# Halo matmuls in 32-row quarters, the first channel piece decoded between the first sums, and the token weights stored by SP behind the later loads

## The chip, the cores and the metric

The kernel runs on one core of a Trainium2 chip. The metric is device time in microseconds; before the change the median of three runs is 2021.88 us (2021.09 to 2022.40). Lines such as L522 are lines of the kernel before; the change moves later lines down, so the same statement can have another number in the changed kernel.

## What is computed

Eight sequences of 4096 tokens with 192 channels go through a causal convolution with seven taps (one softmax-normalized filter for each of eight heads of 24 channels), then through two residual products: over the tokens (4096 to 256 to 4096) and over the channels (192 to 1536 to 192). The weights arrive as 64-bit floats.

```python
w = softmax(weight)                                  # 8 heads x 7 taps
out = einsum('hk,bskhg->bshg', w, windows_of(x))     # causal: six zero rows ahead
xt = out.transpose(0, 2, 1)
h = np.maximum(xt @ w_tok1, 0.0) @ w_tok2
u = out + h.transpose(0, 2, 1)
h2 = np.maximum(u @ w_ch1, 0.0) @ w_ch2
return u + h2
```

## The kernel before

The eight sequences are worked in five groups (1, 1, 2, 2, 2). Only the first sequence and its function `stage1_first` are touched. A row block is 128 tokens; a sequence has 32 of them, in four chunks of eight (`x0`, `xc`).

**Convolution of the first sequence.** For every head a 128 x 128 matrix `band` multiplies a row block (L522), and a second matrix `corner` multiplies the row block ahead of it (L523): only the last six rows of that block, the halo, meet weights other than zero. Both products go over all 128 rows. A chunk therefore takes 16 matmuls in plain float32 (a float32 matmul is two records in the trace). Chunks 1 to 3 load nine row blocks for eight, the first being the halo's. `conv_out` (L525) copies the sums from PSUM to `xc` on ScalarE.

**Decoding.** A 64-bit weight is turned into float32 by an Abs on ScalarE (L196) and four operations on VectorE (L198, L199, L202, L205); pieces that are used in two parts (high and low) get a cast on ScalarE (L211) and a subtraction on VectorE (L212). Sixteen pieces are loaded by SP in a fixed order: eight of the first token weights (t1, kept in `tops`), the first piece of the second token weights (t2 piece 0), three thirds of the first channel weights (w1), three of the second (w2, kept as `w2f`), and t2 piece 1. The raw pieces live in six buffers, so a load waits until the last VectorE operation (L205) on the piece that held its buffer.

**Products of the first sequence.** `mix` (L453) sums `xc` times t1 into two PSUM accumulators; `mix1_done` (L382, L383) makes their parts `h1`; `first_mix` is the call of `mix2` (L920 to L922, sums on VectorE at L935) on the first four row blocks, which needs t2 piece 0; `first_transposed` makes the operand `own` (L984 to L990); `first_channel1` (L1080, Relu L1092) needs w1, `first_channel2` (L1098) w2. The next `mix2` (L924, L925) needs t2 piece 1. The order of all this is written out by hand at the end of `stage1_first` (L572 to L622).

**Stores of that stage.** `xc` goes to DRAM by SP (L538); the decoded t1 goes to DRAM as `t1d` by GpSimd's queue (L445), ahead of `first_channel1`; the next sequences read it from there (L712). SP's queue works in program order: a transfer that waits holds all behind it. The first load of the next sequence (`raw`, L648) takes memory that `tops` held, so it waits for those stores.

Of the kernel before, what the change touches and what calls it, by code (L numbers as in the profile page):

```python
# [139 lines left out]
def conv_mixer_kernel(ctx: ExitStack, tc: tile.TileContext, x, weight, w_tok1, w_tok2, w_ch1, w_ch2, out):  # L140
# [6 lines left out]
    P = 128  # L147
# [241 lines left out]

    def stage1_first(pe, p0, pd, late, load_u, load_next, after, thirds, hooks):
        b = GROUPS[0][0]
        NC = 8
        chunks = [range(s0, s0 + NC) for s0 in range(0, NJ, NC)]
# [24 lines left out]
        t1s = t1d.rearrange("(j p) m -> p j m", p=P)  # L420

        band = p0.tile([P, H, P], F32, name="band")
        corner = p0.tile([P, H, P], F32, name="corner")
        nc.gpsimd.memset(corner, 0.0)

        homes = [(pe if c else p0).tile([P, NC + 1, D], F32, name=f"x0_{c}") for c in range(len(chunks))]
        xcs += [p0.tile([P, NC, D], F32, name=f"xc0_{c}") for c in range(len(chunks) - 1)]
        tops = [p0.tile([P, TJ * JT], F32, name=f"t1_{i}") for i in range(NJ // TJ)]

        def x0_load(c):  # L430
            x0 = homes[c]
            x0s.append(x0)
            j0 = chunks[c].start
            if c == 0:
                nc.gpsimd.memset(x0[:, 0, :], 0.0)
                nc.sync.dma_start(out=x0[:, 1:], in_=xt[:, 0:NC])
            else:
                nc.sync.dma_start(out=x0, in_=xt[:, j0 - 1:j0 + NC])

        def t1_job(i):  # L440
            src = w_tok1.rearrange("(j p) m -> p j m", p=P)[:, quads[i].start:quads[i].stop]
            return dict(src=src, shape=[TJ, JT], top=lambda: tops[i])

        def t1_store(i):
            nc.gpsimd.dma_start(  # L445
                out=t1s[:, quads[i].start:quads[i].stop], in_=tops[i].rearrange("p (j m) -> p j m", m=JT)
            )

# [34 lines left out]
        def make_band():  # L483


            def moved(out, off, hs):
                at0 = P - off
                nc.tensor.matmul(out=out, lhsT=turn[:, at0:at0 + P], rhs=band_r[:, hs], start=True, stop=True)

            halves = [slice(h, h + H2) for h in (0, H2)]  # L490
            for hs in halves:
                v = products.rearrange("p (h c) k -> p h c k", c=BC)
                nc.vector.tensor_tensor(
                    out=v, in0=ones.unsqueeze(1).to_broadcast([BR, H2, BC, K]),
                    in1=cw[:BR, hs].unsqueeze(2).to_broadcast([BR, H2, BC, K]), op=ALU.mult,
                )
                nc.vector.tensor_reduce(
                    out=band_r[:, hs].rearrange("p h c -> p (h c)"), in_=products, axis=AX.X, op=ALU.add
                )
            for hs in halves:  # L500
                ps = ps_x.tile([P, P // BC, H2, BC], F32, name="ps_x")
                for b0 in range(P // BC):
                    moved(ps[:, b0], b0 * BC - HALO, hs)
                nc.scalar.copy(out=band[:, hs].rearrange("p h (b c) -> p b h c", c=BC), in_=ps)
                ps = ps_x.tile([P, H2, BC], F32, name="ps_x")
                moved(ps, P - HALO, hs)
                nc.scalar.copy(out=corner[:, hs, 0:BC], in_=ps)
                if hs.start == 0:
                    keep_busy(9)

        def conv_mm(m):
            c, part = m // 2, m % 2
            x0 = x0s[c]
            n = NC
            for h2 in range(part * H // 4, (part + 1) * H // 4):
                ps = ps_x.tile([P, TT], F32, name="ps_x")
                convs.setdefault(m, []).append((h2, ps))
                for i in range(2):
                    h = 2 * h2 + i
                    o = ps[:, i * n * G:(i + 1) * n * G].rearrange("p (j g) -> p j g", g=G)  # L520
                    hs = slice(h * G, (h + 1) * G)
                    nc.tensor.matmul(out=o, lhsT=band[:, h], rhs=x0[:, 1:, hs], start=True, stop=False)  # L522
                    nc.tensor.matmul(out=o, lhsT=corner[:, h], rhs=x0[:, :n, hs], start=False, stop=True)  # L523

        def conv_out(m):  # L525
            c, part = m // 2, m % 2
# [15 lines left out]
        def begin(n):  # L542
            chains_a.append(dec.a(sts[n], jobs[n]["top"]() if "top" in jobs[n] else None))
# [28 lines left out]
        for n in range(nj - 1):  # L572
            if n + 2 < nj:
                begin(n + 1)
# [6 lines left out]
            if n in (len(quads) - 1, len(quads)):  # L581
                woven(chains.pop(0))
            woven(*chains, split(n - 2) if n > 1 and "top" not in jobs[n - 2] else [])
            if n + 2 == nj:
                begin(n + 1)
            for fn in work.get(n, ()):
                fn()
            if n not in (0, 6, 9):
                next_load()
            if n == 1:  # L590
                x0_load(3)
            if n == 8:
                for c in (3, 0, 1, 2):
                    xc_store(c)
            if n == 7:
                load_u(xcs[0])
            if n == 9:
                late()
        n = nj - 1
        mix1_done(0, accs)  # L600
        woven(split(n - 2))
        hooks[0]()
        hooks[1]()
        woven(chains_a[n - 1][2:], chains_a[n][:2])
# [295 lines left out]
    QB = 32  # L900
    NQ = P // QB

    def mix2(gi, q, t2, u, at_once=False, turned=None):
        nb = len(GROUPS[gi])
        n = nb * D

# [6 lines left out]
        for j in range(TJ):  # L913
# [150 lines left out]
    def first_next(xc):  # L1064
        first["next"] = first_load(xc, TJ)

    def first_mix():
        mix2(0, 0, *first["u"], at_once=True)

    def first_transposed():  # L1070
        first["abc"] = transposed(first["u"][1])
# [98 lines left out]
        queue.dma_start(out=dst[:, js.start:js.stop], in_=osb[:, js.start:js.stop])  # L1170

    hp = None
    pe_ctx, p0_ctx, pd_ctx, ht_ctx = (ExitStack() for _ in range(4))
    pe = pe_ctx.enter_context(tc.tile_pool(name="pe", bufs=1))
    pd = pd_ctx.enter_context(tc.tile_pool(name="pd", bufs=1, side="right"))
    p0 = p0_ctx.enter_context(tc.tile_pool(name="p0", bufs=1, side="right"))

    def first_late():
# [6 lines left out]
    def first_done():  # L1185
# [6 lines left out]

    thirds = [range(p, p + NP // 3) for p in range(0, NP, NP // 3)]
    stage1_first(
        pe, p0, pd, first_late, first_u, first_next, first_done, thirds,
        [first_mix, first_transposed] + [lambda p=p: first_channel1([p]) for p in range(NP)],
    )
    pd_ctx.close()
    t2sp.append(t2s_ctx.enter_context(tc.tile_pool(name="t2s1", bufs=1, side="right", reuse_waits="tile")))

# [203 lines left out]
```

## Time and profile before

| | |
|---|---|
| median of 3 runs | 2021.88 us |
| the profiled execution: its own time, its span | 2020.89 us, 2019.1 us |
| TensorE busy | 2004.4 us, 99% of the span |
| TensorE busy in the first 140 us | 129.81 us |
| VectorE busy in the first 140 us | 114.71 us |
| granted TensorE clock | 1.00 throughout |
| all DMA engines, first 140 us | share 0.79, 257 GB/s |

How to read the lines in the prediction: a timeline row is start, duration, engine, line, operation, output<-inputs, shapes, number merged (x), and in brackets the idle time of the engine ahead of it and what ended it. A row of the chain of waits is start, duration and what the program's end waited on there. A row of the table by windows is the stretch, its length, busy time and number of instructions of PE, weight loads, DVE, ACT, POOL, then the clock, the DMA share (1.0 is all 16 engines; rounding takes it a little above) and GB/s. "SPq" is SP issuing a transfer.

### The profile page before, as it was taken

Reading aid. Unit: us, or ns where it says so; the run is one execution under the profiler, and the core shown is the slowest. Engines: PE = TensorE matmul, PEld = TensorE weight load, DVE = VectorE, ACT = ScalarE, POOL = GpSimd, SP = SyncE. Lnnn points to the kernel's source line nnn. Section 1 sums busy time; section 2 is a strip of 40 time slices with the busy share of each in tenths; the row PEclk is TensorE's granted clock in tenths of the full one; section 3 lists DMA queues with packets and bytes.
Section 4 is the critical chain, followed back from the end, with each engine's and each line's share of the span. In section 5 each row is a group of like instructions: output and inputs, shape, how many; then the busy total and the mean of one; then the engine's idle time right before and its main releaser. Section 6 shows DMA issues by size and latency. Waiting matters only on the chain.

```text
span 2019.1 us, 44729 instructions
## 1 busy us (share of the span) xinstructions
PE 2004.4 (99%) x18667; PEld 1859.3 (92%) x18667; DVE 1506.1 (75%) x3008; ACT 777.5 (39%) x1280; POOL 216.9 (11%) x380
## 2 busy tenths in 40 slices
PE   9899999999999999999999999999999999999999
PEld 9789999999999999998999999999999999999998
DVE  8799998998758998857985689556666666666664
ACT  4676554544333434324333334233233222333322
POOL 0100000001211011100111100111111010011110
PEclk9999999999999999999999999999999999999999
DMA  9855446455455567324654435433223232333310
GB/s 306 285 160 164 137 156 203 153 170 176 138 152 142 160 191 204 115 77 123 170 162 116 116 83 157 148 87 85 54 72 83 71 85 69 77 85 85 85 49 17
DMA packets 280089, 260.93 MB, mean 129 GB/s; under 512 B 188624, under 2 KB 227280, under 8 KB 279888
## 3 DMA queue, kind: packets, MB, share of 16 engines
q1 hardware_dynamic: 257360, 179.80, 31.6%
q0 software_dynamic: 22528, 78.27, 12.9%
q8 instruction: 148, 2.42, 0.5%
q14 instruction: 53, 0.43, 0.1%
HBM read 146.60 MB, written 71.30 MB: 108 GB/s over the span
## 4 chain that ended last, share of the span: by engine, by line
PE 89%; DVE 5%; DMA 3%; SPq 1%; ACT 1%; issue 1%; POOL 0%; ACTq 0%; DVEq 0%
PE ps_x L1080 36%; PE ps_x L1139 23%; PE ps_x L1156 12%; PE ps_x L1157 5%; PE ps_x L959 2%; DVE xc L660 2%; PE ps_a L767 2%; PE ps_a L768 2%; PE ps_a L769 2%; DMA dec_raw<-in_moe_w_tok_dram 1%; DVE hl L1122 1%; PE ps_x L927 1%; PE ps_x L924 1%; PE ps_x L929 1%; PE ps_x L928 1%; PE ps_a L763 1%
## 5 line engine op out<-in xcount | busy, mean ns | idle before, releaser
L1121 ACT ACTIVATE hh<-ps_x 128x512 fp32r<-128x512 f32 x756 | 411.1, 596 | 838.9 <-PE ps_x L1080 838.8
L1122 DVE SCALAR_TENSOR_TENSOR hl<-ps_x,hh 128x512 fp32r<-128x512 f32 x756 | 484.5, 684 | 190.5 <-ACT hh L1121 188.9
L1139 PE MATMUL ps_x<-w,hh 64*128 64x384 f32 x3360 | 481.3, 355 | 0.0
L1139 PE MATMUL ps_x<-w,hl 64*128 64x192 f32 x3360 | 421.2, 247 | 0.0
L660 DVE SCALAR_TENSOR_TENSOR xc<-raw,cw,xc 128x384 f32<-128x384 f32 (+1 forms) x768 | 388.0, 559 | 8.5 <-ACT xc L658 8.5
L1156 PE MATMUL ps_x<-w,hh 128*128 128x384 f32 x1344 | 387.6, 360 | 0.0
L1080 PE MATMUL ps_x<-other,w_hi 64*128 64x512 f32 x1296 | 337.2, 388 | 0.0
L1157 PE MATMUL ps_x<-w,hl 128*128 128x192 f32 x1344 | 336.5, 250 | 0.0
L1080 PE MATMUL ps_x<-own_hi,w_hi 64*128 64x512 f32 x1440 | 332.6, 392 | 1.6 <-ACT own_hi L989 0.6
L1080 PE MATMUL ps_x<-own_lo,w_hi 64*128 64x512 f32 x1440 | 326.1, 387 | 0.1
L1080 PE MATMUL ps_x<-own_hi,w_lo 64*128 64x512 f32 x1440 | 325.7, 387 | 0.0
L1139 PEld LDWEIGHTS ps_x<-w,hl 64*128 64x128 f32 x3360 | 321.3, 188 | 0.9
L1139 PEld LDWEIGHTS ps_x<-w,hh 64*128 64x128 f32 x3360 | 315.4, 184 | 0.9
L1157 PEld LDWEIGHTS ps_x<-w,hl 128*128 128x128 f32 x1344 | 256.6, 191 | 0.0
L1080 PEld LDWEIGHTS ps_x<-other,w_hi 64*128 64x128 f32 x1296 | 235.5, 184 | 22.3
L1156 PEld LDWEIGHTS ps_x<-w,hh 128*128 128x128 f32 x1344 | 252.3, 188 | 0.4 <-DVE hl L1122 0.4
L1080 PEld LDWEIGHTS ps_x<-own_hi,w_hi 64*128 64x128 f32 x1440 | 212.7, 184 | 32.5 <-issue 4.6
L1080 PEld LDWEIGHTS ps_x<-own_lo,w_hi 64*128 64x128 f32 x1440 | 218.4, 184 | 25.3 <-ACT own_lo L990 0.5
L1080 PEld LDWEIGHTS ps_x<-own_hi,w_lo 64*128 64x128 f32 x1440 | 218.2, 184 | 25.2
L1080 PE MATMUL ps_x<-other,w_lo 64*128 64x512 f32 x648 | 181.5, 386 | 0.0
L1147 DVE TENSOR_TENSOR osb<-ps_x,osb 128x192 f32<-128x192 f32 x420 | 150.1, 357 | 25.7 <-DVE osb L1147 0.9
L1145 DVE TENSOR_TENSOR osb<-ps_x,u 128x192 f32<-128x192 f32 x140 | 49.7, 355 | 135.0 <-PE ps_x L1139 135.0
(164 smaller groups left out, 2421.7 us busy)
## 6 DMA issues: line engine op xcount, KB each, us to landing
raw<-in_x_dram SPq DMA_DIRECT2D x56, 672.0 KB, 7.3
t<-t2d SPq DMA_DIRECT2D x64, 512.0 KB, 5.8
u<-xcd SPq DMA_DIRECT2D x62, 384.0 KB, 7.3
xcd<-xc POOLq DMA_DIRECT2D x28, 768.0 KB, 8.0
t<-t1p SPq DMA_DIRECT2D x32, 512.0 KB, 4.5
out_dram<-osb POOLq DMA_DIRECT2D x36, 384.0 KB, 3.4
out_dram<-osb SPq DMA_DIRECT2D x27, 384.0 KB, 3.3
t2d<-stage SPq DMA_DIRECT2D x16, 512.0 KB, 4.9
```

Of the source, the lines that this page charges most:

```text
L660: nc.vector.scalar_tensor_tensor(out=dst, in0=src, scalar=cw[:, h, k:k + 1], in1=dst, op0=ALU.mult, op1=ALU.add)
L767: nc.tensor.matmul(out=ps, lhsT=wh, rhs=xh, start=a, stop=False)
L768: nc.tensor.matmul(out=ps, lhsT=wh, rhs=xl, start=False, stop=False)
L769: nc.tensor.matmul(out=ps, lhsT=wl, rhs=xh, start=False, stop=z)
L1080: nc.tensor.matmul(out=ps, lhsT=w1[w][rows, t[h][2][c], p * P:(p + 1) * P], rhs=t[h][v][rows, c], start=n == 0, stop=n == len(prods) - 1,)
L1121: nc.scalar.activation(out=h["hh", f], in_=ps, func=AF.Relu)
L1122: nc.vector.scalar_tensor_tensor(out=h["hl", f], in0=ps, scalar=0.0, in1=f32(h["hh", f]), op0=ALU.max, op1=ALU.subtract)
L1139: nc.tensor.matmul(out=ps[:, :m], lhsT=h[part, f][ks, ts], rhs=w2[ks, f, :m], start=n == 0 and part == "hh", stop=z and part == "hl",)
L1145: nc.vector.tensor_tensor(out=rows(osb[:, j]), in0=rows(pss[0][:, :D]), in1=tokens(u, i)[:, j], op=ALU.add)
L1147: nc.vector.tensor_tensor(out=osb[:, j], in0=v, in1=osb[:, j], op=ALU.add)
L1156: nc.tensor.matmul(out=ps[:, :2 * D], lhsT=h["hh", f][:, ts], rhs=w2[:, f, :], start=n == 0, stop=False)
L1157: nc.tensor.matmul(out=ps[:, :D], lhsT=h["hl", f][:, ts], rhs=w2[:, f, :D], start=False, stop=z)
```

## The change

Four things are changed, all for the first sequence:

1. The halo has a tile of its own: `halo` holds at partitions 32g to 32g+5 the last six rows of every preceding row block, for head pair g. Four transfers on ScalarE's queue fill it from x (6 x 31 runs of 48 floats each). Chunks load eight row blocks. The `corner` matrices stand in the same quarters, and the eight halo matmuls of a chunk use six rows of one quarter each, four to a round, and follow the eight band matmuls of the chunk.
2. The decode of the first third of w1 no longer stands ahead of `mix1_done`: the loop ends one piece earlier, and the four VectorE operations on that third are put between the four sums of `first_mix` (`between`). The later thirds move back accordingly.
3. The stores of t1 to `t1d` are issued by SP, behind the load of t2 piece 1; they were on GpSimd's queue ahead of `first_channel1`.
4. `tops` and three of the `xc` tiles are in a pool of their own (`p1`), closed after the stage; the stores of `xc` go in the order 0, 3, 1, 2.

```diff
+        halo = p0.tile([P, NJ, 2 * G], F32, name="halo")
+        nc.gpsimd.memset(halo[:, 0], 0.0)
+        for g in range(NQ):
+            nc.scalar.dma_start(
+                out=halo[g * QB:g * QB + HALO, 1:], in_=xt[P - HALO:, :NJ - 1, 2 * g * G:2 * (g + 1) * G]
+            )
...
-                nc.sync.dma_start(out=x0, in_=xt[:, j0 - 1:j0 + NC])
+            nc.sync.dma_start(out=x0, in_=xt[:, chunks[c].start:chunks[c].stop])
...
         def t1_store(i):
-            nc.gpsimd.dma_start(
+            nc.sync.dma_start(
...
-                    nc.tensor.matmul(out=o, lhsT=band[:, h], rhs=x0[:, 1:, hs], start=True, stop=False)
-                    nc.tensor.matmul(out=o, lhsT=corner[:, h], rhs=x0[:, :n, hs], start=False, stop=True)
+                    nc.tensor.matmul(out=sums(ps, i), lhsT=band[:, h], rhs=x0[:, :, hs], start=i == 0, stop=False)
+            if part:
+                for i in range(2):
+                    for g, ps in convs[m - 1] + convs[m]:
+                        rs = slice(g * QB, g * QB + HALO)
+                        nc.tensor.matmul(
+                            out=sums(ps, i), lhsT=corner[rs, g, i],
+                            rhs=halo[rs, chunks[c].start:chunks[c].stop, i * G:(i + 1) * G], start=False, stop=i == 1,
+                        )
...
+        woven(chains_a[nt][2:])
+        late()
+        woven(split(nt))
         mix1_done(0, accs)
-        woven(split(n - 2))
-        hooks[0]()
+        hooks[0](list(chains_a[nt + 1]))
+        woven(split(nt + 1))
+        begin(nt + 2)
+        next_load()
+        woven(chains_a[nt + 2][:2])
         hooks[1]()
...
+        woven(chains_a[nt + 3][2:])
+        next_load()
+        woven(split(nt + 3))
         for i in range(len(quads)):
             t1_store(i)
...
+                if between:
+                    between.pop(0)()
```

The order on VectorE from the end of t2 piece 0 (`dec_top_432`, shape 128x1024) to the first operations on `own_lo`; `dec_top_448` and `dec_top_476` are the first two thirds of w1, L383 is `mix1_done`, L935 the sums of `first_mix`. Before:

```order
L198 TENSOR_SCALAR dec_top_448<-dec_top_448 128x768
L205 SCALAR_TENSOR_TENSOR dec_top_432<-early_raw_353,dec_top_432 128x1024
L199 TENSOR_SCALAR dec_top_448<-dec_top_448 128x768
L202 SCALAR_TENSOR_TENSOR dec_top_448<-dec_raw_376,dec_top_448 128x768
L198 TENSOR_SCALAR dec_top_476<-dec_top_476 128x768
L212 TENSOR_TENSOR t2s_91<-dec_top_432,t2s_91 128x2x512
L205 SCALAR_TENSOR_TENSOR dec_top_448<-dec_raw_376,dec_top_448 128x768
L199 TENSOR_SCALAR dec_top_476<-dec_top_476 128x768
L383 SCALAR_TENSOR_TENSOR h1_486<-ps_a0_133,h1_486 128x192
L383 SCALAR_TENSOR_TENSOR h1_486<-ps_a1_134,h1_486 128x192
L212 TENSOR_TENSOR w1_lo_69<-dec_top_448,w1_hi_68 128x3x256
L935 TENSOR_TENSOR u_446<-ps_x_504,u_446 128x192
```

The same place now (`dec_top_442` is t2 piece 0, `dec_top_458` the first third of w1, L950 the sums):

```order
L205 SCALAR_TENSOR_TENSOR dec_top_442<-early_raw_363,dec_top_442 128x1024
L212 TENSOR_TENSOR t2s_91<-dec_top_442,t2s_91 128x2x512
L383 SCALAR_TENSOR_TENSOR h1_492<-ps_a0_142,h1_492 128x192
L383 SCALAR_TENSOR_TENSOR h1_492<-ps_a1_143,h1_492 128x192
L198 TENSOR_SCALAR dec_top_458<-dec_top_458 128x768
L950 TENSOR_TENSOR u_456<-ps_x_500,u_456 128x192
L199 TENSOR_SCALAR dec_top_458<-dec_top_458 128x768
L950 TENSOR_TENSOR u_456<-ps_x_509,u_456 128x192
L202 SCALAR_TENSOR_TENSOR dec_top_458<-dec_raw_386,dec_top_458 128x768
L950 TENSOR_TENSOR u_456<-ps_x_518,u_456 128x192
L205 SCALAR_TENSOR_TENSOR dec_top_458<-dec_raw_386,dec_top_458 128x768
L950 TENSOR_TENSOR u_456<-ps_x_527,u_456 128x192
```

Six operations on w1 that stood ahead of L383 stand behind it now: four between the sums, two (L198 and L199 of the second third) behind them.

The order on SP from the load of t2 piece 1 (`dec_raw`, 128x2x1024) to the first loads for the next sequence (`raw`, then `t1` read back from `t1d`). Before:

```order
L232 DMA dec_raw_605<-in_moe_w_tok2_dram 128x2x1024
L648 DMA raw0_759<-in_x_dram 128x14x96
L648 DMA raw1_762<-in_x_dram 128x14x96
L712 DMA t1_765<-t1d_72 128x512
L712 DMA t1_767<-t1d_72 128x512
```

And now:

```order
L232 DMA dec_raw_607<-in_moe_w_tok2_dram 128x2x1024
L446 DMA t1d_72<-t1_0_134 128x4x256
L446 DMA t1d_72<-t1_1_135 128x4x256
L446 DMA t1d_72<-t1_2_136 128x4x256
L446 DMA t1d_72<-t1_3_137 128x4x256
L446 DMA t1d_72<-t1_4_138 128x4x256
L446 DMA t1d_72<-t1_5_139 128x4x256
L446 DMA t1d_72<-t1_6_140 128x4x256
L446 DMA t1d_72<-t1_7_141 128x4x256
L661 DMA raw0_770<-in_x_dram 128x14x96
```

The eight stores stand between the last load of the stage and `raw` on the same queue; from the loads of t1 from `t1d` on, the order on every engine is that of before.

More of the change, by code (lines that the diff above doesn't have):

```diff
@@ L388, in mix1_accs, with stage1_first @@
         return [ps_a.tile([P, TT], F32, name=f"ps_a{kc}") for kc in range(KC)]
-    def stage1_first(pe, p0, pd, late, load_u, load_next, after, thirds, hooks):
+    def stage1_first(pe, p0, p1, pd, late, load_u, load_next, after, thirds, hooks):
         b = GROUPS[0][0]
@@ L504, in make_band @@
                 nc.scalar.copy(out=band[:, hs].rearrange("p h (b c) -> p b h c", c=BC), in_=ps)
-                ps = ps_x.tile([P, H2, BC], F32, name="ps_x")
-                moved(ps, P - HALO, hs)
-                nc.scalar.copy(out=corner[:, hs, 0:BC], in_=ps)
+                ps = ps_x.tile([P, 2, 2, BC], F32, name="ps_x")
+                gs = range(hs.start // 2, hs.stop // 2)
+                for n, g in enumerate(gs):
+                    moved(ps[:, n], g * QB, slice(2 * g, 2 * (g + 1)))
+                nc.scalar.copy(out=corner[:, gs.start:gs.stop, :, 0:BC], in_=ps)
                 if hs.start == 0:
@@ L571, in stage1_first @@
         }
-        for n in range(nj - 1):
-            if n + 2 < nj:
-                begin(n + 1)
+        nt = len(quads)
+        for n in range(nt + 1):
+            begin(n + 1)
             if n == 1:
@@ L579, in stage1_first @@
             chains = [chains_a[n - 1][2:] if n else [], chains_a[n][:2]]
-            if n in (len(quads) - 1, len(quads)):
+            if n >= nt - 1:
                 woven(chains.pop(0))
-            woven(*chains, split(n - 2) if n > 1 and "top" not in jobs[n - 2] else [])
-            if n + 2 == nj:
-                begin(n + 1)
+            woven(*chains)
             for fn in work.get(n, ()):
                 fn()
-            if n not in (0, 6, 9):
+            if n not in (0, 6):
                 next_load()
@@ L901, in conv_mixer_kernel, with mix2 @@
     NQ = P // QB
-    def mix2(gi, q, t2, u, at_once=False, turned=None):
+    def mix2(gi, q, t2, u, at_once=False, turned=None, between=()):
         nb = len(GROUPS[gi])
@@ L1065, in first_next, with first_mix @@
         first["next"] = first_load(xc, TJ)
-    def first_mix():
-        mix2(0, 0, *first["u"], at_once=True)
+    def first_mix(between):
+        mix2(0, 0, *first["u"], at_once=True, between=between)
     def first_transposed():
@@ L1172, in conv_mixer_kernel @@
     hp = None
-    pe_ctx, p0_ctx, pd_ctx, ht_ctx = (ExitStack() for _ in range(4))
+    pe_ctx, p0_ctx, p1_ctx, pd_ctx, ht_ctx = (ExitStack() for _ in range(5))
     pe = pe_ctx.enter_context(tc.tile_pool(name="pe", bufs=1))
     pd = pd_ctx.enter_context(tc.tile_pool(name="pd", bufs=1, side="right"))
+    p1 = p1_ctx.enter_context(tc.tile_pool(name="p1", bufs=1, side="right"))
     p0 = p0_ctx.enter_context(tc.tile_pool(name="p0", bufs=1, side="right"))
@@ L1194, in conv_mixer_kernel @@
     stage1_first(
-        pe, p0, pd, first_late, first_u, first_next, first_done, thirds,
+        pe, p0, p1, pd, first_late, first_u, first_next, first_done, thirds,
         [first_mix, first_transposed] + [lambda p=p: first_channel1([p]) for p in range(NP)],
     )
+    p1_ctx.close()
     pd_ctx.close()
```

36 lines of the change are left out of this document (13 added, 23 removed).

## The prediction, made before the changed kernel was run

> **What bounds the kernel now.** The page comes first, then a table by windows to see where TensorE (PE) waits at all.
>
> ```profile
> PE 2004.4 (99%) x18667; PEld 1859.3 (92%) x18667; DVE 1506.1 (75%) x3008; ACT 777.5 (39%) x1280; POOL 216.9 (11%) x380
> ...
> core 0: us, PE busy (x) PEld busy (x) DVE busy (x) ACT busy (x) POOL busy (x), PEclk, DMA share, GB/s
> 3.20:43.10 39.90, 39.90 (x259) 39.11 (x258) 34.15 (x41) 15.38 (x25) 1.91 (x3) 1.00 1.05 346
> 13.20:55.50 42.30, 42.06 (x257) 41.54 (x256) 37.12 (x42) 19.84 (x32) 0.82 (x1) 1.00 1.06 321
> 55.48:88.09 32.61, 27.38 (x189) 21.92 (x189) 24.88 (x35) 18.86 (x29) 7.47 (x10) 1.00 0.84 303
> 110.50:116.20 5.70, 2.91 (x24) 2.30 (x20) 5.05 (x11) 3.74 (x7) 0.00 (x0) 1.00 0.32 92
> 116.20:140.00 23.80, 23.80 (x181) 22.38 (x183) 21.38 (x52) 17.42 (x24) 0.75 (x1) 1.00 0.50 158
> ```
>
> PE is busy for 99% of the span; what it lacks lies almost wholly ahead of 116 us. From there PE never stops, so a change in the first stage is worth what it moves the moment at which PE has the first sequence's operands. From 13 to 55 us PE is full, but so are the 16 DMA engines (1.06), and from 55 to 88 us it idles 5.2 us. The chain of waits of the first 140 us tells what was late:
>
> ```profile
> 13.35 13.84 DMA dec_raw<-in_moe_w_tok_dram
> ...
> 41.27 12.94 DMA dec_raw<-in_moe_w_ch_dram
> 54.32 0.91 ACT dec_top L196
> ...
> 67.81 12.80 DMA dec_raw<-in_moe_w_tok_dram
> 80.63 1.15 ACT dec_top L196
> ...
> 85.77 1.05 ACT t2s L211
> ...
> 86.85 1.24 DVE t2s L212
> ...
> 88.13 0.36 PE ps_x L925
> ```
>
> Three loads bound the stage, each landing 13 us after its issue: a t1 piece, the last third of w1 (its Abs at 54.32 stands on ScalarE ahead of the Relu of the first mix), and t2 piece 1, for which PE waits until 88.13. The mark by which I count is this 88.13 us, the first matmul on the low part of t2 piece 1.
>
> **Part 1: the halo matmuls.**
>
> ```profile
> 13.95 0.49 PE L522 MATMUL ps_x<-x,band 128*128 128x192 f32 x2
> 14.28 0.49 PE L523 MATMUL ps_x<-x,corner 128*128 128x192 f32 x2
> ...
> 49.89 5.36 PE L453 MATMUL ps_a<-u,t 128*128 128x192 f32 x32
> ...
> 65.12 0.85 PE L1080 MATMUL ps_x<-own_hi,w_lo 64*128 64x512 f32 x6
> 65.80 0.85 PE L1080 MATMUL ps_x<-own_lo,w_hi 64*128 64x512 f32 x6
> ```
>
> Starts lie 14.28 - 13.95 = 0.33 us apart, so a matmul (two records) costs 0.33 and the 32 halo matmuls 10.4 us. Four in four quarters cost about one if they run side by side: 2.6 us, 7.8 us off PE. Halves seem to run so: at L1080 six records of 512 columns, on 64 rows each, start every 0.68 us, 0.11 each, where a record of 192 columns on full rows costs 5.36/32 = 0.17 at L453 (in another number format, so this is a hint only). But PE is not alone in its lateness, so the 7.8 us are not the gain. The last 16 matmuls of the mix need the fourth chunk's copies on ScalarE, and those stand behind the Abs of t2 piece 0, which waits for its landing:
>
> ```profile
> 43.12 1.18 ACT L196 ACTIVATE dec_top<-early_raw 128x1024 f32<-128x1024 f32 x1 [3.94 <-DMA early_raw<-in_moe_w_tok_dram]
> 44.19 1.62 ACT L532 COPY u<-ps_x 128x384 f32<-128x384 f32 x4
> ...
> 59.53 1.06 ACT L986 CAST own_hi<-ps_x 128x512 fp32r<-128x512 f32 x2 [3.14 <-PE ps_x L984]
> ...
> 63.41 0.62 ACT L990 CAST own_lo<-own_lo 64x512 fp32r<-64x512 f32 x1
> ...
> 77.05 0.89 ACT L196 ACTIVATE w2f<-dec_raw 128x768 f32<-128x768 f32 x1 [3.75 <-DMA dec_raw<-in_moe_w_ch_dram]
> ...
> 97.06 0.67 ACT L196 ACTIVATE dec_top<-dec_raw 128x512 f32<-128x512 f32 x1
> ```
>
> The copies end at 44.19 + 1.62 = 45.8; the 16 matmuls (5.36) then end at 51.2 instead of 55.25. The landing at 43.1 is the new bound there.
>
> **Part 2: the decode moved behind the first mix.** VectorE's rows:
>
> ```profile
> L198 DVE TENSOR_SCALAR dec_top<-dec_top 128x768 f32<-128x768 f32 x2 | 1.1, 560 | 0.9 <-ACT dec_top L196 0.9
> L199 DVE TENSOR_SCALAR dec_top<-dec_top 128x768 uint32<-128x768 uint32 x2 | 1.1, 553 | 0.0
> L202 DVE SCALAR_TENSOR_TENSOR dec_top<-dec_raw,dec_top 128x768 uint32<-128x768 uint32 x1 | 1.0, 957 | 0.0
> L205 DVE SCALAR_TENSOR_TENSOR dec_top<-dec_raw,dec_top 128x768 uint32<-128x768 uint32 x1 | 1.0, 952 | 0.0
> ...
> 55.48 0.62 DVE L383 SCALAR_TENSOR_TENSOR h<-ps_a,h 128x192 fp32r<-128x192 f32 x2 [0.87 <-ACT h L382]
> ...
> DVE w2f L198 <- ACT w2f L196: 2.3, 1, 2.3
> DVE w_lo L212 <- ACT w_hi L211: 1.7, 3, 0.9
> DVE t2s L212 <- ACT t2s L211: 1.1, 1, 1.1
> ```
>
> The Abs at 54.32 no longer stands ahead of the Relu, so L383 ends at about 51.95 (51.2, Relu 0.3, L383 0.35) instead of 56.10: a list equal to that of 55.48 starts at 51.3. From L383 to t2 piece 1 VectorE worked 24.88 us in 32.61. Six operations on w1 come in from ahead: 2 x 0.56 + 2 x 0.55 + 0.96 + 0.95 = 4.1, so 29.0. Waits that stay: 1.7 and 1.1. A new one: the Abs of the third w1 piece now stands on ScalarE behind the five operations on `own`, which take 63.41 + 0.62 - 59.53 = 4.5 us. By my walk (last sum 56.4; ScalarE casts w1's first third at 56.1, does an Abs to 57.8, `own` to 62.25, the third Abs to 63.1) VectorE runs dry at 61.2 and waits 2.0 us. With 0.7 for gaps between dependent operations: 51.3 + 29.0 + 1.7 + 1.1 + 2.0 + 0.7 = 85.8 against 88.1, **2.3 us earlier**. What hides PE: the first channel product is done by about 75.4, then waits for w2, whose last third VectorE finishes at about 79.6; 16 matmuls of 0.33 end at 84.8. If VectorE had no work, PE's 84.8 would be late next; it is 1 us behind.
>
> **Part 3: the stores of t1 behind the loads.** They leave the queue of transfers that the w2 thirds and t2 piece 1 wait in. The 3.75 us at 77.05 and its echo of 2.3 us on VectorE go; both are already left out of the sum above, in which VectorE's own work is late next. What comes instead: SP issues the eight stores after t2 piece 1, and `raw` and the next t2 pieces are queued behind them.
>
> ```profile
> SPq L648 <- DMA t1d<-t: 11.8, 1, 11.8
> ...
> 59.43 6.13 POOL L445 DMA_DIRECT2D t1d<-t  x8
> ...
> 80.13 6.05 SPq L648 DMA_DIRECT2D raw<-in_x_dram  x2
> 86.29 2.65 SPq L712 DMA_DIRECT2D t<-t1d  x5
> ```
>
> `raw` waited for the stores before too, until 80.13. Now they start at about 69 and, with t2 piece 1, are 5.2 MB; at the 346 GB/s of the first window that is 15 us (SP reaches them when the third w1 piece is decoded, 68.4 by my walk), so `raw` starts at about 84 to 85. The second `raw` waited for VectorE to 86.3, so half of this is made up; the next t2 piece, whose Abs at 97.06 did not wait, may land 0 to 1.5 us late. I take **+0.5**.
>
> **Part 4: the halo transfers.** No transfer on six partitions is in this trace. Four times 186 runs of 192 bytes come in at about 2.3 us on ScalarE's queue. The nearest row is a `raw` load, 1792 runs of 384 bytes:
>
> ```profile
> 81.00:85.00 4.00, 3.83 (x23) 3.84 (x24) 3.21 (x5) 0.77 (x1) 0.10 (x1) 1.00 0.69 172
> ...
> 20.25 0.69 DVE L198 TENSOR_SCALAR t<-t 128x1024 f32<-128x1024 f32 x1 [1.64 <-ACT t L196]
> ```
>
> That is 4 x 0.69 = 2.8 us of 16 engines, so 744 runs cost 1.15 us if all 16 share them, and 16/6 of that, 3.1 us, if only six do. Against it three chunks load a row block less, 295 KB, 0.85 us at 346 GB/s. DMA is full from 3 to 43 us, so the difference, +0.3 to +2.2 us, delays the landing of 43.1 and everything behind it; I take **+1.2**. [...] ScalarE issues four transfers ahead of the Exp of the softmax; the fourth may wait for the first. Until it lands the Exp, the bands and VectorE's first decodes stand behind it; VectorE waits 1.6 us for the third t1 piece at 20.25, so up to that much costs nothing, and what is beyond it falls on the same landing chain that the +0.3 to +2.2 already delays.
>
> **Sum.** -2.3 + 0.5 + 1.2 = -0.6 us. From the windows' last row on, order and work are those of before and PE is full, so this goes to the end; the idle of 110 to 116 us stays. On the profiled execution (2020.89, 1.8 beyond its span, 1.0 below the median) that is 2020.3; on the median of 2021.88, which I forecast, **2021.3 us**. One can tell from no change about 0.2%, 4 us.
>
> **The rivals.**
>
> *The halo costs nothing and the new wait doesn't come* (ScalarE gets the third Abs in early): -2.3 - 0.85 - 2.0 = -5.1, **2016.8 us**. For it: the runs are short, only 143 KB. Against: DMA is full at 1.05, and the order on ScalarE is fixed. Chance 0.13.
>
> *The stores on SP hold up the next sequence.* Before, they took from 59.43 to 80.13, 20.7 us, in company. If they take as long from 69, `raw` starts at 89.7, 9.6 us later than before; some 2 are made up by the gap ahead of 86.3, and the t2 piece at 97.06 comes 7 late, which PE meets at its wait at 116. Less 2.3, plus 1.2: +5.9, **2027.8 us**. It decides when the stores land after about 85; each us past that is a us. For it: nothing else of SP can pass them. Against: the transfers that shared the engines then are over by 69. Chance 0.13.
>
> *The quarters don't run side by side:* PE pays the 10.4 us still, the mix ends at 55.25, and VectorE's list starts 4.05 later: -2.3 + 4.05 + 0.5 = +2.25, with the halo's loads hidden by PE, **2024.1 us**. Against: the 0.11 us of L1080. Chance 0.09.
>
> **How the numbers follow.** Forecast 0.65. Its own range: the halo +0.3 to +2.2, the stores 0 to +1.5, the waits 1 us either way: -3.0 to +2.4, 2018.9 to 2024.3. The quarters' case lies in it. To hold 8 in 10 I widen towards the two others: 2017.6 to 2025.2. Faster by over 0.2% (below 2017.8) is the first rival and little else: 0.14. Slower (above 2025.9) is the second: 0.13. Same: 0.73.
>
> **What would show it.** Right: halo matmuls at about 0.08 us each; PE idle between 20 and 45 us; the second L383 near 53 us; a wait of VectorE for the third Abs of w1 near 63; t2 piece 1 no longer waited for; `raw` issued at 84 to 86. Wrong: the second L383 past 55 (the halo's transfers or the Exp are dearer), `raw` past 88 with PE waiting behind it, or a mark (88.13) that moves by more than 4 us.

## The result and the profile after

The changed kernel takes 2027.97 us, median of 7 runs (2025.9 to 2031.0), beside 2021.83 us for the kernel before in the same session: 6.1 us more, ratio 1.0029 with a 95% interval of 1.0019 to 1.0039. That is slower by 0.3%, with an interval clear of 1, and outside the range given. The profiled execution took 2026.7 us, its span is 2024.9 us, its mean granted clock 0.997. Of all executions behind this document one, of the kernel with the stores alone (e9 below), took 6847.85 us, for a reason that is not known; its ratio leaves it out.

Line numbers up to 400 are those of before; later ones are 1 to 17 higher (halo L533, mix L454, copies L545, stores L446, `raw` L661, the second half of `mix2` L937 and L938, sums L950, channel product L1095). The experiments' kernels shift again by a few.

First the order of time at four points that every trace shows, in us from the start of the profiled execution:

| point on TensorE | before | after | difference |
|---|---|---|---|
| the mark: first matmul on the low part of t2 piece 1 | 88.13 | 88.62 | +0.5 |
| third token mix, the matmul that waits for the low part of the next t2 piece | 116.11 | 120.33 | +4.2 |
| the next channel product | 132.63 | 138.55 | +5.9 |
| the channel product after that | 162.08 | 168.00 | +5.9 |

The loss arises in two stretches, 88 to 120 us and 120 to 139 us, and nothing is added later. The table by windows shows PE in the pieces before and between (stretch, length, busy time of PE, PEld, DVE, ACT, POOL, clock, DMA share, GB/s). After:

```profile
16.00:26.04 10.04, 6.48 (x50) 4.97 (x48) 7.22 (x8) 4.00 (x7) 0.00 (x0) 0.83 1.06 371
26.04:54.43 28.39, 28.39 (x194) 27.49 (x195) 25.33 (x28) 12.57 (x20) 1.36 (x1) 1.00 1.06 306
116.00:120.33 4.33, 0.98 (x5) 0.49 (x4) 3.96 (x9) 2.50 (x4) 0.00 (x0) 1.00 0.40 121
120.33:138.55 18.22, 18.22 (x117) 18.06 (x117) 15.39 (x37) 10.77 (x14) 0.00 (x0) 0.91 0.28 88
```

And the stretch of before that answers to the last row:

```profile
116.11:132.63 16.52, 16.52 (x117) 16.36 (x118) 15.16 (x37) 10.56 (x14) 0.00 (x0) 1.00 0.31 97
```

Three things are to be seen here. PE idles and is slowed from 16 to 26 us, and is then full without a gap until the first mix ends at 54.4. The same 117 matmul records behind 116 us take 18.22 us where they took 16.52: 1.7 us of the loss is clock alone, 0.91 in the mean. And the idle time ahead of it is longer. PE's timeline after has the halo matmuls and both of these waits:

```profile
16.22 0.93 PE L533 MATMUL ps_x<-halo,corner 6*128 6x192 f32 x16
18.68 2.90 PE L528 MATMUL ps_x<-x,band 128*128 128x192 f32 x8 [1.53 <-DMA x<-in_x_dram]
22.82 1.57 PE L528 MATMUL ps_x<-x,band 128*128 128x192 f32 x8 [1.24 <-ACT xc L545]
26.04 3.19 PE L454 MATMUL ps_a<-xc,t 128*128 128x192 f32 x18 [0.79 <-ACT xc L545]
...
120.33 0.36 PE L938 MATMUL ps_x<-h,t2s 128*128 128x192 f32 x1 [3.35 <-DVE t2s L212]
```

The last of them in the timeline of before:

```profile
116.11 0.35 PE L925 MATMUL ps_x<-h,t2s 128*128 128x192 f32 x1 [2.79 <-DVE t2s L212]
```

SP's timeline after shows why it comes late (before, `raw` was issued at 80.13 and the next t2 pieces at 88.99):

```profile
71.43 0.37 SPq L232 DMA_DIRECT2D dec_raw<-in_moe_w_tok_dram  x1
71.85 10.74 SPq L446 DMA_DIRECT2D t1d<-t  x8
89.06 1.25 SPq L661 DMA_DIRECT2D raw<-in_x_dram  x2
90.35 4.50 SPq L725 DMA_DIRECT2D t<-t1d  x5
94.89 0.91 SPq L232 DMA_DIRECT2D dec_raw<-in_moe_w_tok_dram  x2
```

And ScalarE's timeline has the Abs on those pieces, at 97.06 without a wait before:

```profile
102.13 0.67 ACT L196 ACTIVATE dec_top<-dec_raw 128x512 f32<-128x512 f32 x1 [4.60 <-DMA dec_raw<-in_moe_w_tok_dram]
```

For the end of the first mix, five rows of PE, ScalarE and VectorE after. PE starts the last 16 matmuls of the mix without a wait; their operands come from the copies of 46.86, which end at 48.44:

```profile
45.78 1.17 ACT L196 ACTIVATE dec_top<-early_raw 128x1024 f32<-128x1024 f32 x1 [4.14 <-DMA early_raw<-in_moe_w_tok_dram]
46.86 1.58 ACT L545 COPY u<-ps_x 128x384 f32<-128x384 f32 x4
...
49.07 5.36 PE L454 MATMUL ps_a<-u,t 128*128 128x192 f32 x32
...
54.83 0.36 DVE L383 SCALAR_TENSOR_TENSOR h<-ps_a,h 128x192 fp32r<-128x192 f32 x1 [1.30 <-ACT h L382]
...
66.22 0.56 DVE L198 TENSOR_SCALAR dec_top<-dec_top 128x768 f32<-128x768 f32 x1 [1.83 <-ACT dec_top L196]
```

### The profile page after: what moved, and what is told of

It reads as the page before. It is cut to its first block, busy times and chain, and to the rows that moved or that the text cites. A ratio compares the mean times of both kernels' runs of the same rounds, so it can differ in the third digit from the quotient of the medians.

```text
span 2024.9 us, 44731 instructions
## 1 busy us (share of the span) xinstructions
PE 2004.5 (99%) x18671; PEld 1853.6 (92%) x18671; DVE 1505.3 (74%) x3008; ACT 777.6 (38%) x1280; POOL 211.7 (10%) x372
## 4 chain that ended last, share of the span: by engine, by line
PE 92%; DVE 4%; DMA 1%; SPq 1%; ACT 1%; issue 0%; POOL 0%; DVEq 0%; ACTq 0%
PE ps_x L1095 37%; PE ps_x L1154 23%; PE ps_x L1171 13%; PE ps_x L1172 6%; PE ps_x L974 2%; PE ps_a L780 2%; PE ps_a L781 2%; PE ps_a L782 2%; DVE xc L673 1%; PE ps_x L937 1%; PE ps_a L454 1%; PE ps_x L940 1%; DMA dec_raw<-in_moe_w_tok_dram 1%; PE ps_x L942 1%; PE ps_x L941 1%; PE ps_a L776 1%
## 5 line engine op out<-in xcount | busy, mean ns | idle before, releaser
L1095 PE MATMUL ps_x<-own_hi,w_hi 64*128 64x512 f32 x1440 | 334.9, 394 | 4.2 <-DVE osb L1118 1.3
L1095 PE MATMUL ps_x<-other,w_hi 64*128 64x512 f32 x1296 | 337.3, 388 | 0.0
L1095 PE MATMUL ps_x<-own_hi,w_lo 64*128 64x512 f32 x1440 | 327.7, 388 | 0.0
L1095 PE MATMUL ps_x<-own_lo,w_hi 64*128 64x512 f32 x1440 | 327.5, 387 | 0.0
L1095 PEld LDWEIGHTS ps_x<-other,w_hi 64*128 64x128 f32 x1296 | 235.6, 184 | 23.0 <-issue 0.3
L1095 PEld LDWEIGHTS ps_x<-own_hi,w_hi 64*128 64x128 f32 x1440 | 213.2, 184 | 37.4 <-issue 4.6
L1095 PEld LDWEIGHTS ps_x<-own_hi,w_lo 64*128 64x128 f32 x1440 | 219.1, 185 | 26.0 <-DVE w_lo L212 0.5
L1095 PEld LDWEIGHTS ps_x<-own_lo,w_hi 64*128 64x128 f32 x1440 | 219.3, 185 | 25.5
L1095 PE MATMUL ps_x<-other,w_lo 64*128 64x512 f32 x648 | 181.5, 386 | 0.0
```

The costliest lines, as they stand in the source:

```text
L1095: nc.tensor.matmul(out=ps, lhsT=w1[w][rows, t[h][2][c], p * P:(p + 1) * P], rhs=t[h][v][rows, c], start=n == 0, stop=n == len(prods) - 1,)
```

## The experiments

All are medians of 5 to 11 executions, timed in five sessions beside the kernel before, whose medians lie between 2021.19 and 2021.87 us; "difference" is against that median of the same session. Where two kernels of different sessions are compared below, both the plain difference of their medians and the one by this column are given, since they differ by up to 0.6 us.

| kernel | median us | difference | ratio, 95% interval |
|---|---|---|---|
| the change | 2027.97 | +6.1 | 1.0019 to 1.0039 |
| stores back (e1) | 2026.26 | +5.1 | 1.0011 to 1.0029 |
| old halo (e2) | 2028.93 | +7.7 | 1.0021 to 1.0048 |
| decode's place, with the fourth item (e4) | 2024.48 | +3.3 | 1.0006 to 1.0023 |
| stores alone (e9) | 2023.77 | +2.6 | 1.0003 to 1.0021 |
| no halo transfers (e5) | 2027.42 | +5.6 | 1.0018 to 1.0036 |
| w1 ahead (e6) | 2026.52 | +4.9 | 1.0017 to 1.0038 |
| PE kept busy (e7) | 2026.02 | +4.4 | 1.0013 to 1.0030 |
| stores back, w1 ahead (e8) | 2024.43 | +2.8 | 1.0005 to 1.0023 |
| copies ahead (e15) | 2026.39 | +4.9 | 1.0016 to 1.0034 |
| copies ahead, stores halved, PE busy (e16) | 2020.93 | -0.6 | 0.9988 to 1.0006 |
| before, stores halved (e10) | 2021.23 | -0.4 | 0.9992 to 1.0009 |
| before, stores early (e11) | 2022.91 | +1.0 | 0.9998 to 1.0015 |
| the same, PE busy (e12) | 2021.04 | -0.8 | 0.9984 to 1.0002 |
| before, PE busy (e13) | 2019.86 | -2.0 | 0.9982 to 1.0000 |
| before, stores halved, PE busy (e14) | 2019.68 | -1.8 | 0.9983 to 1.0000 |

**Which part loses: e1, e2, e4, e9.** The traces pointed at the stores (theory A), with the halo transfers as rival B. The first kernel undoes the stores:

```diff
         def t1_store(i):
-            nc.sync.dma_start(
+            nc.gpsimd.dma_start(
...
         load_next(xcs[0])
+        for i in range(len(quads)):
+            t1_store(i)
         after()
```

> The eight stores of the first token weights go back to GpSimd's queue and to their old place in the program; the halo matmuls in quarters and the decode between the sums stay. Theory A (the stores on SP hold up the next sequence's input and, behind it, the next low token weights): the next input is issued by SP near 80 us and not at 89.1, the wait of 4.6 us before the Abs at 102 us goes, and the time is 2021.5 to 2023.5 us. Rival B (the halo transfers and the front of the program, 0 to 55 us, make the loss): the stores matter little and the time stays at 2026 to 2028 us.

Theory A did not hold: `raw` was issued at 79.20 and no wait for the t2 piece was left, and yet the time fell by only 1.7 us (2026.26; 1.1 by the column). That lies in rival B's range, which the next kernel rules out. PE's row of this kernel at the third mix, and the window behind it, show a cause that the expectation did not have:

```profile
118.87 0.53 PE L938 MATMUL ps_x<-h,t2s 128*128 128x192 f32 x1 [2.79 <-DVE t2s L212]
```

```profile
120.00:124.00 4.00, 4.00 (x17) 4.00 (x16) 3.23 (x10) 0.00 (x0) 0.00 (x0) 0.50 0.00 0
```

PE waits 2.79 us there, exactly as in the profile of before, but here the clock falls to 0.50, and the 117 records up to the next channel product take 19.34 us instead of 16.52. The wait itself is over 2.76 us later than before, as much as the mark (90.90). The kernel with the old halo puts back L522, L523 and the nine-block loads of before:

> The halo matmuls of before (full height, with the x tiles one row-block longer and no halo transfers) stand in the changed kernel; stores on SP and decode between the sums stay. Theory A: the loss is in the stores, so 2025.5 to 2028 us, with the next input still issued by SP past 87 us. Rival B: the loss was in the halo, so 2020.5 to 2022.5 us. Either way the high token weights' Abs (first piece) should fall back from 45.8 to near 43.1 us, and PE have some 8 us more of halo matmuls.

Theory B falls: without the new halo the change is no faster (2028.93, even above the range of theory A). Then the two other parts: e4 has the halo and the stores of before, and keeps the fourth item of the change (the pool `p1` and the order of the `xc` stores) beside the decode; e9 is the kernel before with one edit (the stores on SP, after the last split):

> Of the three parts only the decode between the first mix's sums is left: halo matmuls and stores as before. Both A and B say that this part costs nothing: 2020.5 to 2022.5 us. If it is the decode's place that loses (rival C), the time is above 2025 us here.

> The kernel before with one edit: the eight stores of the first token weights go to SP's queue, behind the load that follows the last channel piece. Theory A: the next input is issued past 87 us instead of near 82, the next low token weights come some 4 to 5 us later, and the time is 2025 to 2028 us. Rival B: 2021 to 2023 us, since the next input has slack.

Each of them loses, 3.3 and 2.6 us, which add up to 5.9 of the 6.1; that the sum fits does not show that the parts add, and undoing them one by one gives back less. That the decode's place costs nothing was wrong, though 2024.48 us is under the 2025 us that rival C asked for. VectorE's timeline in e4 shows how it loses:

```profile
51.10 1.23 DVE L212 TENSOR_TENSOR t2s<-dec_top,t2s 128x1024 fp32r<-128x1024 f32 x1 [1.11 <-ACT t2s L211]
54.08 0.36 DVE L383 SCALAR_TENSOR_TENSOR h<-ps_a,h 128x192 fp32r<-128x192 f32 x1 [1.75 <-ACT h L382]
56.68 0.36 DVE L383 SCALAR_TENSOR_TENSOR h<-ps_a,h 128x192 fp32r<-128x192 f32 x1 [2.24 <-ACT h L382]
```

VectorE works in order here: it stands 1.75 and 2.24 us before the two L383, until PE ends the mix, and the decode that used to fill this time is queued behind them. The channel product then starts at 63.58 us instead of 60.17, and the mark comes at 90.79, 2.7 us late. Some 0.9 us of this is that the second L383 ends later in this execution (57.04, before 56.10), the rest arises in the list behind it. After the wait at the third mix the clock falls here too (0.65 from 120 to 124 us), and the stretch to the next channel product takes 18.10 us instead of 16.52. No run has the fourth item alone.

In e9 the mark comes 2.65 us **early** (85.48): the stores no longer share the transfers with the last third of w2, and the wait of 3.75 us at its Abs is gone. Then SP's queue and ScalarE take it back:

```profile
68.71 11.19 SPq L445 DMA_DIRECT2D t1d<-t  x8
86.47 1.25 SPq L648 DMA_DIRECT2D raw<-in_x_dram  x2
87.76 4.71 SPq L712 DMA_DIRECT2D t<-t1d  x5
92.51 0.91 SPq L232 DMA_DIRECT2D dec_raw<-in_moe_w_tok_dram  x2
...
99.98 0.66 ACT L196 ACTIVATE dec_top<-dec_raw 128x512 f32<-128x512 f32 x1 [5.58 <-DMA dec_raw<-in_moe_w_tok_dram]
```

The wait at the third mix ends at 118.16 instead of 116.11 (+2.05), and the next channel product starts at 137.09 instead of 132.63 (+4.5): the clock (0.57 and 0.58 in the windows from 116 to 124 us) adds 2.4 there, in an execution that took 2025.29 us, 1.5 over the median of this kernel. The median, 2023.77, lies between the two ranges that were expected.

**The decode's place, the clock, and where to put the stores: e6, e7, e8, e10.** e6 moves the first third of w1 back ahead of the mix's end:

```diff
         woven(split(nt))
+        woven(chains_a[nt + 1])
         mix1_done(0, accs)
-        hooks[0](list(chains_a[nt + 1]))
+        hooks[0]([])
```

> The changed kernel with one move: the four VectorE operations of the first w1 third (with their ACT steps) stand ahead of the two L383 steps that wait for the first mix, not between its sums behind them. Theory D (the changed order lost because VectorE stands idle for the mix's end, 50.9 to 54.8 us, with this decode queued behind): the decode fills that idle stretch, the channel matmuls start at 58.5 to 59.5 us instead of 61.1, the mark comes at 86 to 87 instead of 88.6, and the time is 2025 to 2026.5 us, some 2 us under the changed kernel. Rival (the decode's place costs nothing, the mark is set by the landing of w2): mark and time stay within 0.7 us, 2027.5 to 2028.5 us.

> Stores back on GpSimd at their old place and the first w1 third decoded ahead of the first mix's end, so that of the change the halo quarters are what is left. Theories A and D add up: 2.5 us off the 2026.3 us of the kernel with the stores back, so 2023 to 2024.5 us; if the halo quarters alone were worth what they take off PE, it would be under 2020 us; if the six-row transfers cost what they delay (2.7 us at 45 us) on the path that ends last, 2023.5 us.

In e6 VectorE is busy up to the mix's end:

```profile
52.38 0.55 DVE L198 TENSOR_SCALAR dec_top<-dec_top 128x768 f32<-128x768 f32 x1
52.96 0.56 DVE L199 TENSOR_SCALAR dec_top<-dec_top 128x768 uint32<-128x768 uint32 x1
53.56 0.96 DVE L202 SCALAR_TENSOR_TENSOR dec_top<-dec_raw,dec_top 128x768 uint32<-128x768 uint32 x1
54.55 0.96 DVE L205 SCALAR_TENSOR_TENSOR dec_top<-dec_raw,dec_top 128x768 uint32<-128x768 uint32 x1
55.43 0.62 DVE L383 SCALAR_TENSOR_TENSOR h<-ps_a,h 128x192 fp32r<-128x192 f32 x2
```

but the second L383 ends 0.9 us later than in the change (56.05 against 55.19), the mark comes 0.9 us earlier (87.76), and 1.4 us of the time come back (1.3 by the column); between e1 and e8, which differ by the same move and share no session, 1.8 (2.3). Both are what theory D says in kind, at the lower end of its size, and each alone is less than the intervals can tell apart.

e8 has little of the change left but the halo, and is still 2.8 us over the kernel before, clear of noise. This is not the price of the halo, though, for its decode stands directly ahead of L383, and PE waits for that:

```profile
57.79 0.36 PE L935 MATMUL ps_x<-h,t2s 128*128 128x192 f32 x1 [2.55 <-DVE h L383]
```

e7 gives PE something to do in its wait:

```diff
+                    if nxt == (0, 2):
+                        ps = ps_x.tile([P, TT], F32, name="ps_x")
+                        for k in range(22):
+                            nc.tensor.transpose(out=ps[:, k % TJ * P:(k % TJ + 1) * P], in_=ident, identity=ident)
                     mix2(*nxt, *loaded, turned=z)
```

> The changed kernel with 22 transposes of the identity, whose result nobody reads, on PE ahead of the third token mix's second half (at 116 us), where PE stands idle for 3.4 us until the low token weights are split. Theory E (that idle stretch makes the granted clock fall to 0.60 at 120 to 124 us, and that costs 1.6 us): the clock there stays above 0.9, the stretch from the third mix's low matmul to the next channel matmuls takes 16.5 us instead of 18.2, and the time is 2026 to 2027 us. Rival (the clock falls for another reason): it falls all the same, 2028 us or a little more.

The two windows, of the change:

```profile
120.00:124.00 4.00, 3.67 (x16) 3.67 (x16) 3.54 (x10) 0.68 (x1) 0.00 (x0) 0.60 0.01 4
```

and of e7:

```profile
120.00:124.00 4.00, 3.23 (x25) 2.98 (x23) 3.93 (x9) 0.94 (x2) 0.00 (x0) 1.00 0.12 47
```

The clock stays at 1.00 from 112 to 128 us, and the median falls by 1.9 us (1.8 by the column), within what the intervals leave open: theory E, which two more pairs below bear out. The profiled execution does not show the gain, for in it the clock fell elsewhere, and it took 2026.71 us, as long as that of the change:

```profile
108.00:112.00 4.00, 3.73 (x18) 2.97 (x20) 4.00 (x11) 3.30 (x8) 0.91 (x1) 0.57 0.63 157
```

e10 has the stores alone, halved around the load of t2 piece 1:

> The kernel before with the eight stores on SP's queue, four ahead of the load of the low token weights and four behind it, so that the first four go out while the transfer engines stand a third idle (60 to 72 us with all eight behind). Theory A: the next input is issued near 82 us and the next low token weights at 87 to 89 us instead of 92.5, no wait is left before their Abs, and the mark keeps the 2.6 us that the stores' new queue gained (85.5 us): 2019 to 2021.5 us. Rival: the load of the low token weights comes later by as much as the four stores take (some 5 us), the mark falls back to 88 us or later, and the time is 2023 us or more.

```profile
64.92 3.78 SPq L445 DMA_DIRECT2D t1d<-t  x4
68.82 0.97 SPq L232 DMA_DIRECT2D dec_raw<-in_moe_w_tok_dram  x1
69.83 6.61 SPq L445 DMA_DIRECT2D t1d<-t  x4
84.50 1.25 SPq L650 DMA_DIRECT2D raw<-in_x_dram  x2
85.79 4.71 SPq L714 DMA_DIRECT2D t<-t1d  x5
90.55 1.13 SPq L232 DMA_DIRECT2D dec_raw<-in_moe_w_tok_dram  x2
```

The mark keeps its gain (85.79), the next t2 pieces are issued at 90.55, 1.6 us after before and 2 us ahead of e9, later than expected; the 2.6 us that e9 loses become -0.4.

**The halo transfers, earlier stores, and PE kept busy elsewhere: e5, e11, e12, e13.**

> The changed kernel without the four halo transfers: the halo tile holds zeros, so the convolution of the first sequence lacks the six rows ahead of each block. All matmuls stay. Theory F (the six-row transfers delay every landing of the first stage by 2.7 us, and that eats what the quarters take off PE): the x tiles land 2 to 3 us earlier, PE's waits at 16 to 26 us shrink, the high token weights' Abs goes from 45.8 to about 43 us, the first mix ends 2 to 3 us earlier, and the time is 2024.5 to 2026.5 us. Rival (PE's waits there come from the copies of the sums on ACT, behind the weights' Abs, and the mix's end doesn't move): 2027 to 2028.5 us.

Theory F is not borne out. The Abs on t2 piece 0 came at 44.16 instead of 45.78, and the time stayed at 2027.42 us; PE waits as before, only for another thing:

```profile
21.45 2.36 PE L524 MATMUL ps_x<-x,band 128*128 128x192 f32 x8 [2.97 <-ACT xc L541]
...
25.34 7.20 PE L450 MATMUL ps_a<-xc,t 128*128 128x192 f32 x32
```

But this profile is of a long execution (2029.11 us, mean clock 0.995), and the second row shows a part of it: 32 records took 7.20 us (clock 0.50 from 24 to 28 us) where those of the change took 5.47 at 26.04 (clock 1.00), and PE reached the last 16 matmuls of the mix at 50.10 instead of 49.07. What the transfers cost at a full clock stays open.

> The kernel before with the eight stores on SP's queue, but four ahead of the last w2 load and four ahead of the load of the low token weights, so that they fill the 0.35 to 0.44 of transfer time that the kernel with the halved stores shows at 60 to 68 us. Theory A: all stores have landed by 76 us, the next input is issued at 76 to 80 us and not at 84.5, the next low token weights at 86 to 88 us instead of 90.6; the mark stays at 85 to 87 us, and the time is 2018.5 to 2020.5 us. Rival: the last w2 load comes later by what the stores take, the mark is at 88 us or more, 2021.5 to 2023 us.

Here the rival was nearer: t2 piece 1, on the same queue, was issued at 72.15 instead of 67.81, and PE stands 3.01 us for it ahead of a mark at 89.04.

> The kernel with the stores early on SP, and 22 transposes of the identity (no one reads the result) on PE ahead of the third token mix's second half. Theory E: the clock stays near 1.00 there, and the time is 1 to 2 us under that of the kernel with the early stores: 2017 to 2019 us. Rival: the same time, or up to 0.5 us more.

> The kernel before with the same 22 transposes at the same place. Its profile shows no fall of the clock there, but its runs range from 2019 to 2024.5 us with a mean clock of 1.000 to 0.997. Theory E: part of its runs do lose to a fall there; the median goes down by 0.5 to 1.5 us, to 2020 to 2021 us, and the highest time falls. Rival: the median stays within 0.4 us of the kernel before.

Theory E held in both: 1.9 us (to 2021.04, above the range of 2017 to 2019, since the early stores had come out higher) and 2.0 us. With the transposes the kernel before runs from 2019.1 to 2021.1 us, without them, in the same session, from 2019.3 to 2025.3, with mean clocks down to 0.997. So it very likely lost the clock there in a part of its runs too, though no profile shows such a run.

**The copies ahead: e15, e16, e14.** What was open was where PE's 7.8 us go. In e15 the copies on ScalarE stand one or two weight pieces earlier; PE's order is unchanged:

```diff
-        behind = {1: [0], 2: [1], 3: [2, 3], 5: [4, 5], 7: [6, 7]}
+        behind = {0: [0, 1], 2: [2, 3], 4: [4, 5], 6: [6, 7]}
```

> The changed kernel with the copies of the first sequence's convolution sums one or two weight pieces earlier on ACT (L545 of each block of eight ahead of the Abs of t1 pieces 2, 4, 6 and of the high token weights, not behind them); PE's order is the same. Theory G (what the quarters take off PE is lost because PE then waits for these copies, which stand behind an Abs that waits for its landing): PE's waits at 16 to 26 us go, the first mix ends at 50.5 to 52.5 us instead of 54.4, VectorE's list behind it starts as much earlier, the mark is at 86 to 87 us, and the time is 2024.5 to 2026.5 us. Rival (the transfers bound the first mix's end all the same): the mix ends at 54 us or later, and the time stays at 2027 to 2028.5 us.

ScalarE's and VectorE's rows:

```profile
17.22 1.63 ACT L545 COPY xc<-ps_x 128x384 f32<-128x384 f32 x4 [0.93 <-PE ps_x L533]
...
42.02 1.63 ACT L545 COPY u<-ps_x 128x384 f32<-128x384 f32 x4
...
53.71 0.61 DVE L383 SCALAR_TENSOR_TENSOR h<-ps_a,h 128x192 fp32r<-128x192 f32 x2
```

The first copies come 5 us sooner, PE's waits for them between 16 and 26 us go (one for x, 1.70 us, stays), and L383 now waits for VectorE's own split of t2 piece 0, not for PE. PE reaches the last 16 matmuls at 47.24 instead of 49.07. The mark is at 87.52, the time 1.6 us lower (1.2 by the column): theory G in kind, by half its size, and within what the intervals leave open.

> The kernel with the copies ahead, with two more edits: four of the stores go ahead of the load of the low token weights (still on SP), and the 22 transposes that nobody reads keep PE busy ahead of the third token mix's second half. If theories A, E and G add up, 1.5 and 1.9 us go off the time of the kernel with the copies ahead: 2021 to 2023 us, so that the whole change, mended at three places, is level with the kernel before. Rival (they hide each other): 2024 us or more.

> The kernel before with the stores halved around the load of the low token weights on SP (nothing else of the change), and the 22 transposes that nobody reads ahead of the third token mix's second half. Theories A and E: the stores' gain of 0.8 us up to the third mix is kept and no clock is lost behind it, so 0.5 to 1 us under the kernel before with the transposes: 2018.9 to 2019.6 us. Rival (next input late, as at 84.5 us, costs it later): 2020 us or more.

The mended change (2020.93, just under its range) is level with the kernel before, 7.0 us under the change (6.7 by the column); e15, e7 and e1 alone gave 1.6, 1.9 and 1.7, together 5.2 (4.1 by the column, and e1 puts the stores back where e16 halves them). That the three repairs bring the change back to the kernel before is shown; how the 7.0 us divide among them is not, since a lower clock joins in all of them (a mean of 0.995 to 0.997 in the profiled executions of e15, e7, e1 and e16). And one of the repairs, the transposes, helps the kernel before as well: like for like, against 2019.86 (e13) and 2019.68 (e14, same session), the mended change is still 1.1 to 1.3 us longer, which the intervals leave open. Against the kernel before with PE kept busy the halved stores are worth nothing (2019.68, between the two ranges expected, and 2019.86). These two are the fastest, by 0.1%, which is under the 0.2% that I can tell.

## Why the prediction was wrong

**Part 1, the halo matmuls: the bound was the wrong one.** The quarters run side by side, as said: 16 records in 0.93 us, 0.12 us for a matmul instead of 0.33, where 0.08 was expected; that takes 6.8 us off PE, not 7.8. The step that failed is "the 16 matmuls (5.36) then end at 51.2 instead of 55.25. The landing at 43.1 is the new bound there." It looked at the last 16 matmuls and at what stands ahead of their operands, and not at what stands ahead of them on PE. What PE gained on the first two chunks, and 2 us more, it lost again ahead of 26.04 us: 3.6 us in waits for x and for copies that are queued behind an Abs whose weights have not landed, and some 2 us at a clock of 0.83. From 26.04 it had 28.39 us of matmuls to do and did them in 28.39. It reached the last 16 at 49.07, not at 45.8. The operands alone would have been late as well: their copies ended at 48.44, because the Abs on t2 piece 0 stood at 45.78 and not at 43.12 (Part 4). So the two bounds lay 0.6 us apart, and lifting one alone brings little, as e5 and e15 did. The second L383 came at 54.83, not at 53.

**Part 2, the decode: the sum's start, not its terms.** The wait for the third Abs of w1 is there (1.83 us at 66.22, 2.0 predicted), t2 piece 1 is no longer waited for, as said. From the end of the second L383 to the mark it took 33.4 us, 33.9 predicted. But that end came at 55.19, 3.2 us later than 51.95, since the list starts when PE lets it. The change puts the decode behind two steps that wait for the mix's end, and so leaves empty on VectorE what it filled before (waits of 1.75 + 2.24 us in e4, 0.87 in the profile of before); with the fourth item this costs 3.3 us in e4, and putting it back returned 1.3 to 2.3, where I had a gain of 2.3.

**Part 3, the stores: the term was mis-sized, and it is the largest error.** `raw` was expected at 84 to 85 and the t2 piece's Abs 0 to 1.5 us late; `raw` was issued at 89.06 and the Abs ran 5.1 us late. SP reached the stores at 71.85, not at 69. `raw` was then 8.9 us late; half of that was made up, as I had it, but the five t1 loads behind took 4.50 us to issue instead of 2.65, and the next t2 pieces were issued 5.9 us late. So the sign that was named for being wrong, `raw` past 88 with PE waiting behind it, came true: between the mark and the wait at 116 us 3.7 us were lost, where the sum had 0.5. The rival named almost these numbers (89.7, 7 us late, 2027.8 us), and that is a trap: its time fits to 0.2 us and its mechanism is real, but putting the stores back returned only 1.1 to 1.7 us. The same move gives 2.3 us ahead of the mark (90.90 in e1, 88.62 in the change), which I had counted as already hidden. The rival's 7 us were 3.7, the 1.1 us that it took off ahead of the mark were a loss of 0.5, and it had no term for the clock's 1.7: the fit is luck.

**Part 4, the halo transfers: too small, and not alone on the path.** Over the profiles the Abs on t2 piece 0 stands at 44.0 to 46.9 us with the transfers (seven kernels, mean 45.5) and at 42.6 to 44.9 with the old halo (nine, mean 43.6): 1.9 us, nearer to my bound of 2.2 than to the 1.2 taken. That bound was my estimate for the case that only six engines carry the halo's runs, and no run shows the term: which engines carried them, no trace tells, and what the traces show in its place is the 1.9 us. That the time does not hang on this delay alone is what e5 says, with the reserve made there. Whether the whole halo part gains or loses by itself is not settled: e1 against e4, of one session, says +1.8 us, the change against e2 -1.0 (-1.6 by the column), both within the intervals.

**The sum: "PE is full, so this goes to the end".** It went to the end, and on the way the wait at 116 us, which I let stay as it was, grew from 2.79 to 3.35 us, and 1.7 us of clock came on top. No term stood for that. In the profiled executions the parts are these: up to the mark +0.5 us where -1.1 was forecast (-2.3 + 1.2), from there to the end of the wait +3.7 where 0.5 was, behind it +1.7 where nothing was. The errors are 1.6, 3.2 and 1.7 us, together the 6.5 between -0.6 and +5.9.

## What to carry to other kernels

When work is taken off an engine, ask where that engine can use the time: up to the next place where it waits for others, the gain becomes idle time (here 6.8 us came off TensorE, and it reached the last 16 matmuls of the mix 0.8 us sooner, at 49.07 instead of 49.89), and only what is queued behind its last wait is worth the full amount. An operation that is put behind one that waits gives up the cover which that wait had been (1.75 and 2.24 us on VectorE in e4, 0.87 before); on an engine that works in order, as VectorE did there, price the waiting instruction's new time first, and then the list. When a rival's number fits the result, undo its part alone before believing it: here it fitted to 0.2 us, and undoing it gave back 1.1 to 1.7 of 6.1.

## What the runs showed of the hardware

Behind a wait of TensorE of 2.8 to 3.4 us its granted clock fell in some executions and not in others: after 2.79 us the clock was 1.00 in the profile of before and 0.50 (120 to 124 us) in e1, after 3.35 us 0.60 in the change. The cost is 1.7 us here (18.22 against 16.52 for the same matmuls), 2.4 in e9, 2.8 in e1. Why the clock fell behind one wait of 2.79 us (e1) and not behind another as long (before), and whether the short gaps around the wait count too, no run here shows. Twenty-two transposes that nobody reads, in the wait, kept the clock behind it at 1.00 (116 to 128 us) in the profiles of e7, e12 and e13 and took 1.8 to 2.0 us off the medians of these three kernels, the kernel before among them, whose runs then spread over 2.0 us instead of 6.0. The intervals of each pair overlap; that all three agree, and the clock in the windows, is what the reading rests on. The clock also falls in other places, for instance to 0.83 from 16 to 26 us after the change, around waits of 1.53, 1.24 and 0.79 us; which waits lower it, these runs do not settle.

Six rows of 32-row quarters, four at a time into four accumulators, cost 0.93 us for eight float32 matmuls of 192 columns, 0.12 us each, a third of the full-height price (0.33 us each before).
